# A reload that counted as a reader, the place of the second mixing, and one filter block evacuated by VectorE

## Chip, cores and metric

The kernel runs on one core of a Trainium2 chip. The metric is the device time of one execution in microseconds (us); a version is judged by the runs in the fast state only (here: within 1.5% of that kernel's fastest run), and all runs quoted here are of that state. A profile is one execution taken by the hardware profiler. Its span (about 2 us shorter than the time) is what the timelines count from.

## The reference, cut to what matters

```python
x = A_q                                             # [1, 2048, 640] bf16
g = sigmoid((x * gate_w).sum(-1, keepdims=True))
a = A(x, k, v, shift_k, ssm_k, ssm_D)               # 4-tap shift of k, times v, then a causal convolution
                                                    # of length 2048 over the sequence (FFT of length 4096), times q
b = B(x, w1, b1, w2, b2)                            # the MLP: layernorm, two matmuls over the sequence with a GELU between
return g * a + (1 - g) * b
```

The kernel does the FFT as matmuls with sine tables (TensorE) and butterflies ("mixing", VectorE). The sequence is in two halves, so almost everything in A exists twice.

Of the kernel before, what the change touches and what calls it, by code (L numbers as in the profile page):

```python
# [13 lines left out]
ALU = mybir.AluOpType  # L14
# [4 lines left out]
class _Tracker:  # L19
# [231 lines left out]
        self.dma_cnt[name] = 0  # L251

    def dma(self, stream, out_ap, in_ap, semname, transpose=False, noncontig=False, accum=False, wait=()):
        reads = [in_ap] + ([out_ap] if accum else []) + list(wait)
        writes = [out_ap]
        acc = self.pre(stream, reads, writes)
        engobj = self.eng[stream]
        sem = self.dma_sems[semname]
        if transpose:
            ins = engobj.dma_start_transpose(out_ap, in_ap)  # L260
        elif accum:
            ins = engobj.dma_start(out_ap, in_ap, accum_op=ALU.add, max_dma_last_dim=2560)  # L262
        elif noncontig:
            with self.nc.allow_non_contiguous_dma(reason="tiny"):
                ins = engobj.dma_start(out_ap, in_ap)
        else:
            ins = engobj.dma_start(out_ap, in_ap)
        ins.then_inc(sem, 16)
        self.dma_cnt[semname] += 16
        v = self.dma_cnt[semname]  # L270
        self.dma_hist[(semname, v)] = dict(self.known[stream])
        src = ("dma", semname, v)
        for reg, mode in acc:
            self.add_record(reg, mode, src)
        return v
# [234 lines left out]
def _build(nc, A_q, A_k, A_v, A_shift_k, A_ssm_k, A_ssm_D, B_x, B_w1, B_b1, B_w2, B_b2, gate_w, out):  # L510
    Bsz, S, D = A_q.shape
# [9 lines left out]
    with ExitStack() as es:  # L521
# [129 lines left out]
        def act(o, i, func, bias=None, scale=None, acc=None, vt=None, prio=None, name="act"):  # L651
            kw = {}
            rr = []
            nap = 0
            for k_, v_ in (("bias", bias), ("scale", scale)):
                if v_ is not None:
                    kw[k_] = v_
                    if isinstance(v_, bass.AP):
                        rr.append(v_)
                        nap += 1  # L660
            ww = [o]
            if acc is not None:
                kw["accum_out"] = acc
                ww.append(acc)

            def emit(s):
                src = i(s) if vt is not None else i
                return T.op("ACT", lambda e: e.activation(o, src, func, **kw), rr + [src], ww)  # L668
            return SC.add("ACT", act_dur(n_of(o), nap), emit, rr if vt is not None else rr + [i], ww, prio=prio, vt=vt, name=name)
# [31 lines left out]
        def dma(o, i, nbytes, stream="SP", prio=None, sem=None, rate=365.0, chain=False, **kw):  # L701
            if sem is None:
                sem = f"d{ndma[0]}"
                ndma[0] += 1
            if sem not in T.dma_sems:
                T.add_dma_sem(sem, es.enter_context(nc.semaphore(f"s_{sem}")))
            rd = [i] + ([o] if kw.get("accum") else []) + list(kw.get("wait", ()))
            o_ = SC.add(stream, nbytes / rate / 1000.0, lambda s: T.dma({"QA": "ACT"}.get(stream, stream), o, i, sem, **kw), rd, [o], prio=prio, lat=-1.0, name="dma")
            if chain:
                if last[0] is not None:  # L710
                    o_.after.add(last[0])
                last[0] = o_
            return o_
# [125 lines left out]
        def transp(h, db):  # L839
            vt = _VT("cv")  # L840
            items = []
            for kt in range(2):
                for p in range(4):
                    o = (lambda s, j=4 * kt + p: s[:, 128 * j:128 * j + 128])
                    dfold = h == 0 and kt == 0 and p == 0
                    if dfold:
                        items.append((o, ident[0:1, :], Drow[0:1, 128 * db:128 * db + 128], True, False))
                    items.append((o, V(ssm, db * S + 1024 * h + 4 * kt + p, [[8, 128]]), ident[:, :], not dfold, True))
            m_ = mms(vt, (spin(SPIN[db]) if h == 0 else []) + items, name="wtr")
            m_.dur = 0.5  # L850
            o_ = act(V(wT, 2 * h * SL + 128 * db, [[SL, 2], [D, 4], [1, 128]]), (lambda s: s[:, :].rearrange("q (a b c) -> q a b c", a=2, b=4)), ACT.Copy, vt=vt, name="wT")
            if h == 0:
                o_.after.add(sins[0 if db == 0 else 2])
# [85 lines left out]
        MIXP = 330  # L939
        LNA = 8  # L940
        lnlast = []
        kfirst = []
        KFP = (0, 5, 10, 15)
        srcW = lambda h: (lambda kt, p, ci: wT[:, 2 * h + kt, p, 320 * ci:320 * ci + 320])
        for h in range(2):
            for db in range(ND):
                transp(h, db)
            if h == 0:
                consts()
            if h in (1,):  # L950
                fwd_even(srcW(h), h, C[h], 1.0 / 1024.0, h == 1, "W")
            for p in (PORD if h not in (1,) else PORD[2:]):
                if h == 0 and p in (1, 3):
                    sins[p].prio = SC.ops[-1].idx - (16.5 if p == 1 else 8.5)
                fwd(srcW(h), h, p, C[h], p, 1.0 / 1024.0, "W", (lambda c, k2: False) if h == 0 else (lambda c, k2: c == 1))
            if h == 0:
                for t in range(8):
                    ln_tile(t // 4, t % 4)
                for t in range(8, 12):
                    ln_tile(t // 4, t % 4)  # L960
                lnlast.append(SC.ops[-1])
                ln_scale(0, LNA)
                ln_apply(0, LNA)
                lnlast.append(SC.ops[-1])
                for t in range(12, 16):
                    for o_ in ln_tile(t // 4, t % 4):
                        o_.after.update(lnlast[-1:])
                ln_scale(LNA, 16)
                ln_apply(LNA, 16)
                lnlast.append(SC.ops[-1])  # L970
                for g0 in KFP:
                    tt("POOL", KF[:, g0:g0 + 20 // len(KFP), :, :], V(cw, 7 * g0, [[7, 20 // len(KFP)], [1, 7], [0, 32]]), V(m32, 0, [[0, 20 // len(KFP)], [0, 7], [1, 32]]), ALU.mult, xr=[pv3] if g0 == 0 else []).after.update(kfirst[:1])
                    kfirst.append(SC.ops[-1])
                for hk in range(2):
                    k_turn(hk)
                mixing(C[0], SS, 0, fine=True, prio=MIXP)
            else:
                mixing(C[1], C[0], 0, conj=True, prio=MIXP)
# [152 lines left out]
        def H(hs, c):  # L1131
            h, s = hs
            return V(h, s * SL + 1280 * c, [[SL, 2], [1, 1280]])
# [54 lines left out]
                dma(comp(V1[g], i, 0), tmp, 128 * 5120, stream="POOL", prio=0, accum=True)  # L1188


        def invmix(Ya, Yb, sc, z0, z2):
            def sl(h, s):
                return V(h, s * SL, [[1, SL]])

            def pr(h, s, rev=False):
                return V(h, s * SL + (1280 if rev else 0), [[-1280 if rev else 1280, 2], [1, 1280]])
            (ha, sa), (hb, sb), (hs, ss) = Ya, Yb, sc
            tt("DVE", sl(hs, ss), sl(ha, sa), sl(ha, sa + 1), ALU.add)
            tt("DVE", sl(ha, sa), sl(ha, sa), sl(ha, sa + 1), ALU.subtract)
            tt("DVE", sl(hs, ss + 1), sl(hb, sb), sl(hb, sb + 1), ALU.add)  # L1200
            tt("DVE", sl(hb, sb), sl(hb, sb), sl(hb, sb + 1), ALU.subtract)
            tt("DVE", sl(ha, sa + 1), sl(hs, ss), sl(hs, ss + 1), ALU.add)
            tt("DVE", sl(hb, sb + 1), sl(hs, ss), sl(hs, ss + 1), ALU.subtract)
            oA = V(hs, ss * SL, [[SL + 1280, 2], [1, 1280]])
            oB = V(hs, (ss + 1) * SL, [[-1280, 2], [1, 1280]])
            tt("DVE", oA, pr(ha, sa), pr(hb, sb, True), ALU.add)
            tt("DVE", oB, pr(ha, sa), pr(hb, sb, True), ALU.subtract)
            return {0: (ha, sa + 1), 2: (hb, sb + 1), 1: (hs, ss), 3: (hs, ss + 1)}

        def inverse(h, Z):  # L1210
# [51 lines left out]
        acc_dma(A1[1], V1[1])  # L1262
        acc_dma(A1[0], V1[0])
        chained(product, A0[1], A0[1], V0[1], H(V0[1], 0))
        for kt in range(2):
            dma(q_hi[:, kt, :, :], dr(A_q, 512 * kt * D, [[4 * D, 128], [1, 4 * D]]), 128 * 5120, wait=[H(A0[1], 1)])
        chained(product, A0[0], A0[0], V0[0])
        for kt in range(2):
            dma(q_lo[:, kt, :, :], dr(A_q, (1024 + 512 * kt) * D, [[4 * D, 128], [1, 4 * D]]), 128 * 5120).after.add(w2last)
        Z0 = invmix(A0[0], A0[1], C3a, None, None)  # L1270
        inverse(0, Z0)
        Z1 = invmix(A1[0], A1[1], (SS, 0), None, None)
        inverse(1, Z1)

        SC.run()
# [35 lines left out]
```

## The kernel before: what the change touches

The kernel records every operation first. A list scheduler, working with modelled durations, then fixes the order on each engine; a tracker adds the semaphore waits from what each operation reads and writes. So a declared read acts twice: in the order and in the waits.

```python
# tracker: what a DMA is recorded to read
def dma(self, stream, out_ap, in_ap, semname, transpose=False, noncontig=False, accum=False, wait=()):
    reads = [in_ap] + ([out_ap] if accum else []) + list(wait)
    writes = [out_ap]
    acc = self.pre(stream, reads, writes)            # waits on the issuing stream
    # ... start the DMA
    for reg, mode in acc:
        self.add_record(reg, mode, src)              # later writers of these regions wait for this DMA
```

```python
# scheduler: the same regions once more
rd = [i] + ([o] if kw.get("accum") else []) + list(kw.get("wait", ()))
o_ = SC.add(stream, nbytes / rate / 1000.0, lambda s: T.dma(..., **kw), rd, [o], prio=prio, lat=-1.0, name="dma")
```

```python
def transp(h, db):                                   # half h, block db of 5: 8 transposes on TensorE
    # ...
    o_ = act(V(wT, ...), (lambda s: ...), ACT.Copy, vt=vt, name="wT")      # ScalarE evacuates 128x1024 fp32

def invmix(Ya, Yb, sc, z0, z2):                      # eight instructions of 128x2560
    (ha, sa), (hb, sb), (hs, ss) = Ya, Yb, sc
    tt("DVE", sl(hs, ss), sl(ha, sa), sl(ha, sa + 1), ALU.add)             # 1
    tt("DVE", sl(ha, sa), sl(ha, sa), sl(ha, sa + 1), ALU.subtract)        # 2
    tt("DVE", sl(hs, ss + 1), sl(hb, sb), sl(hb, sb + 1), ALU.add)         # 3
    tt("DVE", sl(hb, sb), sl(hb, sb), sl(hb, sb + 1), ALU.subtract)        # 4  overwrites A0's second half
    tt("DVE", sl(ha, sa + 1), sl(hs, ss), sl(hs, ss + 1), ALU.add)         # 5  -> first inverse block
    tt("DVE", sl(hb, sb + 1), sl(hs, ss), sl(hs, ss + 1), ALU.subtract)    # 6  -> second inverse block
    tt("DVE", oA, pr(ha, sa), pr(hb, sb, True), ALU.add)                   # 7  -> third
    tt("DVE", oB, pr(ha, sa), pr(hb, sb, True), ALU.subtract)              # 8  -> fourth

chained(product, A0[1], A0[1], V0[1], H(V0[1], 0))   # ends in an accumulating DMA into H(A0[1], 1)
for kt in range(2):                                  # reload q into q_hi; "wait" holds it behind that DMA
    dma(q_hi[:, kt, :, :], dr(A_q, ...), 128 * 5120, wait=[H(A0[1], 1)])
# ...
Z0 = invmix(A0[0], A0[1], C3a, None, None)
inverse(0, Z0)                                       # uses q_hi
Z1 = invmix(A1[0], A1[1], (SS, 0), None, None)
inverse(1, Z1)                                       # uses q_lo
```

## Time and profile before

| | before |
|---|---|
| time, median of six runs (lowest to highest) | 183.76 us (183.45 to 185.66) |
| span of the profile | 181.9 us |
| TensorE busy, VectorE busy | 173.2 us, 171.3 us |
| Z0's first instruction starts | 143.64 |
| Z0's sixth instruction ends, second inverse block starts | 158.11, 158.25 |
| TensorE idle just before that | 1.74 us |
| last VectorE instruction ends | 179.65 |

The first three runs, with a median of 184.76 us, were the ones known when the prediction was made. The lines themselves, and how to read them, are in the prediction.

### The profile page before, as it was taken

What the parts mean: (1) busy time and instruction counts of PE and PEld (TensorE: products, weight loads), DVE (VectorE), ACT (ScalarE), POOL (GpSimd) and SP (SyncE); (2) the same over time, 40 slices, a digit from 0 to 9 for tenths busy, and PEclk for the clock granted to TensorE, in tenths of its full rate; (3) what the DMA queues carried; (4) which work ended last, traced back from release to release, by engine and by line L of the source; (5) the groups of instructions that cost most, each with busy time, mean ns of one, the idle gap of its engine ahead of it and who ended that gap; (6) DMA issues with size and microseconds to landing.
All of it is one profiled execution on the core that took longest, in us unless ns stands there. A gap on an engine that the chain in (4) does not pass through costs nothing.

```text
span 181.9 us, 3336 instructions
## 1 busy us (share of the span) xinstructions
PE 173.2 (95%) x1380; PEld 129.3 (71%) x1381; DVE 171.3 (94%) x203; ACT 116.9 (64%) x176; POOL 45.3 (25%) x42
## 2 busy tenths in 40 slices
PE   7969998899999999999999999999999999699993
PEld 2636785586778677776777778888888887477772
DVE  7999895999999999999999899999999996999974
ACT  5798998899898999428999911322313225156760
POOL 4089404580000055000241101205252000041300
PEclk9999999999999999999999999999999999999999
DMA  5999999999999999998499799797999999146787
GB/s 159 376 410 370 389 269 200 266 397 300 213 262 269 176 279 234 230 229 220 110 269 260 147 180 349 143 216 236 189 194 227 204 241 416 66 76 144 123 258 271
DMA packets 38542, 43.51 MB, mean 239 GB/s; under 512 B 15867, under 2 KB 31360, under 8 KB 38528
## 3 DMA queue, kind: packets, MB, share of 16 engines
q1 hardware_dynamic: 33296, 32.16, 58.0%
q0 software_dynamic: 5200, 11.14, 35.2%
q8 instruction: 11, 0.18, 0.4%
q14 instruction: 3, 0.02, 0.0%
q10 hardware_dynamic: 32, 0.01, 0.0%
HBM read 25.87 MB, written 2.62 MB: 157 GB/s over the span
## 4 chain that ended last, share of the span: by engine, by line
PE 47%; ACT 19%; DVE 18%; DMA 11%; issue 3%; SPq 0%; DVEq 0%
PE pp L293 47%; DVE C L624 10%; DMA C<-SS 5%; DMA q_hi<-in_A_q_dram 5%; ACT C L668 5%; ACT gq L668 5%; DVE tm L624 4%; ACT FTB L668 3%; ACT wT L668 3%; DVE q_hi L624 2%; ACT ksh L668 2%; ACT GT L668 2%; DVE SS L624 1%; ACT L668 1%; DVE O L680 0%
## 5 line engine op out<-in xcount | busy, mean ns | idle before, releaser
L293 PE MATMUL pp<-X,ring 128*128 128x320 bf16 x384 | 55.4, 299 | 0.0
L624 DVE TENSOR_TENSOR C<-C 128x2560 bf16<-128x2560 bf16 (+2 forms) x37 | 54.5, 1521 | 0.3 <-DMA q_hi<-in_A_q_dram 0.3
L293 PE MATMUL pp<-GT,W 128*128 128x320 bf16 x384 | 52.8, 299 | 0.0
L293 PEld LDWEIGHTS pp<-GT,W 128*128 128x128 bf16 x384 | 43.5, 113 | 8.7
L293 PEld LDWEIGHTS pp<-X,ring 128*128 128x128 bf16 x384 | 37.4, 98 | 14.4
L668 ACT ACTIVATE C<-pp 128x640 bf16<-128x640 f32 x64 | 40.4, 724 | 4.7 <-PE pp L293 4.7
L668 ACT ACTIVATE O<-pp,c,omg 128x640 bf16<-128x640 f32 x15 | 13.2, 883 | 33.8 <-PE pp L293 33.8
L262 POOL DMA_DIRECT2D C<-C x8 | 10.9, 1610 | 41.9 <-DVE C L624 38.4
L293 PE MATMUL pp<-wT,FTB 128*128 128x320 bf16 x112 | 17.2, 299 | 2.6 <-ACT wT L668 1.5
L668 ACT ACTIVATE cgb<-pp,gg 128x640 bf16<-128x640 f32 x16 | 12.7, 793 | 8.5 <-PE pp L293 8.5
L293 PEld LDWEIGHTS pp<-wT,FTB 128*128 128x128 bf16 x112 | 10.5, 98 | 7.9 <-ACT wT L668 2.0
L668 ACT ACTIVATE GT<-pp,cc 128x640 bf16<-128x640 f32 x12 | 9.5, 795 | 9.0 <-PE pp L293 9.0
L293 PE MATMUL pp<-C,FTB 128*128 128x320 bf16 x96 | 13.5, 299 | 1.7 <-DVE C L624 1.7
L624 DVE TENSOR_TENSOR tm<-C,C 128x2560 bf16<-128x2560 bf16 (+1 forms) x7 | 14.3, 2057 | 0.0
L920 DVE BATCH_NORM_STATS2 stats<-X 128x6 f32<-128x320 bf16 x32 | 13.5, 462 | 0.0
L293 PEld LDWEIGHTS pp<-C,FTB 128*128 128x128 bf16 x96 | 9.3, 98 | 5.6 <-issue 2.0
L624 DVE TENSOR_TENSOR SS<-C 128x2560 bf16<-128x2560 bf16 x8 | 11.8, 1486 | 1.3 <-DMA C<-C 1.3
L262 POOL DMA_DIRECT2D C<-q_hi x6 | 5.9, 977 | 27.7 <-DVE C L624 13.2
L262 POOL DMA_DIRECT2D O<-q_hi x4 | 4.8, 1200 | 28.5 <-DVE q_hi L624 28.5
L668 ACT ACTIVATE gq<-gq 128x640 bf16<-128x640 bf16 x16 | 11.8, 739 | 0.0
L624 DVE TENSOR_TENSOR C<-tm 128x2560 bf16<-128x2560 bf16 (+1 forms) x9 | 10.6, 1191 | 0.1
L668 ACT ACTIVATE wT<-pp 128x1024 bf16<-128x1024 f32 x10 | 9.7, 1043 | 1.0 <-PE pp L293 1.0
(73 smaller groups left out, 200.4 us busy)
## 6 DMA issues: line engine op xcount, KB each, us to landing
ring<-in_B_w_dram SPq DMA_DIRECT2D x12, 512.0 KB, 9.9
W<-in_B_w_dram SPq DMA_DIRECT2D x12, 512.0 KB, 6.3
C<-C POOLq DMA_DIRECT2D x8, 640.0 KB, 10.5
X<-in_A_q_dram SPq DMA_DIRECT2D x4, 640.0 KB, 8.4
kn<-in_A_k_dram SPq DMA_DIRECT2D x4, 640.0 KB, 9.1
out_dram<-O SPq DMA_DIRECT2D x7, 320.0 KB, 3.0
C<-SS POOLq DMA_DIRECT2D x3, 640.0 KB, 11.5
ssm<-in_A_ssm_k_dram SPq DMA_DIRECT2D x3, 512.0 KB, 6.8
```

Of the source, the lines that this page charges most:

```text
L262: ins = engobj.dma_start(out_ap, in_ap, accum_op=ALU.add, max_dma_last_dim=2560)
L293: ins = self.nc.tensor.matmul(ps_ap, lhsT=lhsT, rhs=rhs, start=start, stop=stop, skip_group_check=True)
L624: o_ = SC.add(eng, d, lambda s: T.op(eng, lambda e: e.tensor_tensor(o, a, b, op), rd, [o]), rd, [o], prio=prio, name="tt")
L668: return T.op("ACT", lambda e: e.activation(o, src, func, **kw), rr + [src], ww)
L920: ops.append(SC.add("DVE", 0.38, (lambda o, i: lambda s: T.op("DVE", lambda e: e.bn_stats(o, i), [i], [o]))(o, i), [i], [o]))
```

## The change

The intent: hold the reload of q_hi back as before, but only on the stream that issues it; keep the second mixing (Z1) behind the first (Z0); and give VectorE the last filter block while GpSimd computes the second half of the layernorm's reciprocal square roots ("the roots", rstd in the lines).

```diff
     def dma(self, stream, out_ap, in_ap, semname, ..., wait=()):
-        reads = [in_ap] + ([out_ap] if accum else []) + list(wait)
+        reads = [in_ap] + ([out_ap] if accum else [])
         writes = [out_ap]
+        if wait:
+            self.pre(stream, list(wait), [])         # waits on the issuing stream, nothing recorded
         acc = self.pre(stream, reads, writes)
...
-            rd = [i] + ([o] if kw.get("accum") else []) + list(kw.get("wait", ()))
+            rd = [i] + ([o] if kw.get("accum") else [])
...
+            if h == 1 and db in [4]:
+                ow = V(wT, 2 * h * SL + 128 * db, [[SL, 2], [D, 4], [1, 128]])
+                def emit(s):
+                    src = s[:, :].rearrange("q (a b c) -> q a b c", a=2, b=4)
+                    return T.op("DVE", lambda e: e.tensor_copy(ow, src), [src], [ow])
+                SC.add("DVE", dve_dur(1024, 1), emit, [], [ow], prio=2, vt=vt, name="wTd").after.add(stlast[-1])
+                return
...
-        def invmix(Ya, Yb, sc, z0, z2):
+        def invmix(Ya, Yb, sc, bfirst=False, behind=None):
+            n0 = len(SC.ops)
...
+            for (hy, sy), k in (((hb, sb), 1), ((ha, sa), 0)) if bfirst else (((ha, sa), 0), ((hb, sb), 1)):
+                tt("DVE", sl(hs, ss + k), sl(hy, sy), sl(hy, sy + 1), ALU.add)
+                tt("DVE", sl(hy, sy), sl(hy, sy), sl(hy, sy + 1), ALU.subtract)
...
+            for o_ in SC.ops[n0:]:
+                o_.after.update(behind or ())
...
+        lastacc = SC.ops[-1]
-            dma(q_hi[:, kt, :, :], ..., wait=[H(A0[1], 1)])
+            dma(q_hi[:, kt, :, :], ..., wait=[H(A0[1], 1)]).deps.add(lastacc)
...
+        Z0 = invmix(A0[0], A0[1], C3a)
+        z0last = SC.ops[-1]
         inverse(0, Z0)
+        Z1 = invmix(A1[0], A1[1], (SS, 0), False, [z0last])
```

The flag bfirst is false in both calls, so of the mixing only the rule "behind" is new.

More of the change, by code (lines that the diff above doesn't have):

```diff
@@ L941, in _build @@
         lnlast = []
+        stlast = []
         kfirst = []
@@ L967, in _build @@
                         o_.after.update(lnlast[-1:])
+                stlast.append(SC.ops[-1])
                 ln_scale(LNA, 16)
@@ L1197, in invmix @@
             (ha, sa), (hb, sb), (hs, ss) = Ya, Yb, sc
-            tt("DVE", sl(hs, ss), sl(ha, sa), sl(ha, sa + 1), ALU.add)
-            tt("DVE", sl(ha, sa), sl(ha, sa), sl(ha, sa + 1), ALU.subtract)
-            tt("DVE", sl(hs, ss + 1), sl(hb, sb), sl(hb, sb + 1), ALU.add)
-            tt("DVE", sl(hb, sb), sl(hb, sb), sl(hb, sb + 1), ALU.subtract)
+            for (hy, sy), k in (((hb, sb), 1), ((ha, sa), 0)) if bfirst else (((ha, sa), 0), ((hb, sb), 1)):
+                tt("DVE", sl(hs, ss + k), sl(hy, sy), sl(hy, sy + 1), ALU.add)
+                tt("DVE", sl(hy, sy), sl(hy, sy), sl(hy, sy + 1), ALU.subtract)
             tt("DVE", sl(ha, sa + 1), sl(hs, ss), sl(hs, ss + 1), ALU.add)
@@ L1264, in _build @@
         chained(product, A0[1], A0[1], V0[1], H(V0[1], 0))
+        lastacc = SC.ops[-1]
+        assert lastacc.eng == "POOL"
         for kt in range(2):
-            dma(q_hi[:, kt, :, :], dr(A_q, 512 * kt * D, [[4 * D, 128], [1, 4 * D]]), 128 * 5120, wait=[H(A0[1], 1)])
+            dma(q_hi[:, kt, :, :], dr(A_q, 512 * kt * D, [[4 * D, 128], [1, 4 * D]]), 128 * 5120, wait=[H(A0[1], 1)]).deps.add(lastacc)
         chained(product, A0[0], A0[0], V0[0])
@@ L1269, in _build @@
             dma(q_lo[:, kt, :, :], dr(A_q, (1024 + 512 * kt) * D, [[4 * D, 128], [1, 4 * D]]), 128 * 5120).after.add(w2last)
-        Z0 = invmix(A0[0], A0[1], C3a, None, None)
+        Z0 = invmix(A0[0], A0[1], C3a)
+        z0last = SC.ops[-1]
         inverse(0, Z0)
-        Z1 = invmix(A1[0], A1[1], (SS, 0), None, None)
+        Z1 = invmix(A1[0], A1[1], (SS, 0), False, [z0last])
         inverse(1, Z1)
```

## The prediction

> **What bounds the kernel now.** I read the page first, for who is busy, and then only the two places that the change touches. Part 1 of the page of the kernel before:
>
> ```profile
> PE 173.2 (95%) x1380; PEld 129.3 (71%) x1381; DVE 171.3 (94%) x203; ACT 116.9 (64%) x176; POOL 45.3 (25%) x42
> ```
>
> TensorE and VectorE are both nearly full in a span of 181.9 us, so nothing can be gained but the gaps of these two, and closing a gap of one helps only while the other does not stand in the way. Next, therefore, the list of waits, for TensorE and then VectorE:
>
> ```profile
> PE pp L293 <- DVE C L624: 1.7, 1, 1.7
> PE pp L293 <- ACT wT L668: 1.5, 1, 1.5
> DVE X L639 <- POOL rstd L624: 2.7, 2, 2.1
> DVE SS L624 <- DMA C<-C: 1.3, 1, 1.3
> DVE C L624 <- DMA q_hi<-in_A_q_dram: 0.3, 1, 0.3
> ```
>
> TensorE's largest gap is 1.74 us, one wait for VectorE; its second, 1.55 us for wT, ends at 13.6 us in the trace, in the first half of the filter, which the change does not touch. The chain that ended last, from 133 us on in the order of time, tells why TensorE waited there:
>
> ```profile
> 133.98 9.76 DMA C<-SS
> ...
> 144.19 9.53 DMA q_hi<-in_A_q_dram
> ...
> 153.81 4.31 DVE C L624 x3
> 158.12 0.14 issue
> 158.25 20.82 PE pp L293 x152
> ```
>
> The reload of q_hi lands at 153.72; only then VectorE runs three instructions, and after the third TensorE starts and never stops again until 0.55 us of VectorE end the work. The last timeline is that of VectorE from 143 us on (start, length, what, idle time before):
>
> ```profile
> 143.64 4.30 DVE L624 TENSOR_TENSOR C<-C 128x2560 bf16<-128x2560 bf16 x3
> 147.85 1.49 DVE L624 TENSOR_TENSOR SS<-C 128x2560 bf16<-128x2560 bf16 x1
> 149.25 1.48 DVE L624 TENSOR_TENSOR C<-C 128x2560 bf16<-128x2560 bf16 x1
> 152.01 1.49 DVE L624 TENSOR_TENSOR SS<-C 128x2560 bf16<-128x2560 bf16 x1 [1.28 <-DMA C<-C]
> 153.81 4.30 DVE L624 TENSOR_TENSOR C<-C 128x2560 bf16<-128x2560 bf16 x3 [0.30 <-DMA q_hi<-in_A_q_dram]
> ```
>
> I read this against the code of invmix, which has eight instructions of this size for each half. The outputs to SS are the first and third of the second half (Z1); those to C are the first half (Z0) and Z1's second. The order is Z0's 1, 3 and 2; Z1's first; Z0's fifth (TensorE's inverse starts at 150.92 on it); Z1's third; Z0's fourth; Z1's second; Z0's sixth, for which TensorE waits. So the sixth of Z0 comes ninth. It was pushed back because the program counts the reload of q_hi as a reader of A0's second half, which Z0's fourth overwrites: a wait that no data need, since the reload reads the input in HBM.
>
> **What the Trainium skill says.** (1) "DMA: Bandwidth & Descriptors", Anatomy of one DMA: DMA engines do not wait on semaphores; the issuing sequencer does, before dispatch. So the wait that delays the reload can be put on the issuing stream alone. The trace agrees: the SP queue shows 11.8 us waiting on C<-SS, and the reload is issued at 143.80, right after C<-SS lands at 143.74. (2) "VectorE: DVE Perf Modes", The TRN2 errata: a PSUM to SBUF instruction costs 120 cycles plus its elements at 0.96 GHz on VectorE, 172 plus its elements at 1.2 GHz on ScalarE. For 1024 fp32 columns that is an estimate of 1.19 us and 1.00 us. The trace has ScalarE's at 1.04 us (4.70 us for five in a row, 0.94 each); it has no such VectorE copy, only 320-column PSUM instructions with a second operand at 552 ns, where the formula gives 458. I take 1.2 to 1.3 us. (3) "GPSIMD Engine Reference", Specifications: VectorE and GpSimd contend when VectorE runs a two-port mode or has two SBUF inputs. A copy from PSUM is neither, so the roots should keep their 1.66 us; no row of this trace shows such a pair. (4) "TensorE: Matmul & The Clock Gate", Part 1: back-to-back warm matmuls take N / 2.4 GHz plus 2.5 ns, 136 ns for 320 columns. The trace agrees: 16 of them from 150.92 to 153.10 are 136 ns each.
>
> **The change, part by part.**
>
> *Reload wait.* The wait stays on the issuing stream (same gate, same 143.8) but the reload no longer counts as a reader. Z0's fourth no longer waits. Removed: the 0.30 us wait and, more, the detour by which Z1's instructions stood before it.
>
> *Mixing order.* The flag bfirst is false in both calls, so the pairs stay in the old order. What is new is that all of Z1 must be placed after the start of Z0's eighth. Z0 then runs straight through. Instructions of 128x2560 follow one another at 1.43 us (4.30 for three). From 143.64: the fifth still ends near 150.7, the sixth at 143.64 + 6 x 1.42 = 152.2 instead of 158.1, the seventh 153.6, the eighth 155.0. Nothing is added: it is the same 16 instructions. Z1's third moves from 152 to after 156, so its 1.28 us wait for C<-C, which landed at 152, is gone too.
>
> TensorE after that: from 150.92 to its last matmul it has 152 + 24 + 16 = 192 left, of which 64 are MLP matmuls that can go anywhere, 192 x 0.136 = 26.1 us, so 177.0 at the best against 179.08 now. That includes the 1.74 us gap and small ones.
> VectorE after that: from 143.64 to 179.65 it has 33.1 us of busy time in 36.0, so about 176.8 at the best. It has to make Z0, four products with q_hi (0.75 each) and five of Z1 before TensorE's second inverse: 155.0 + 3.0 + 7.1 = 165.1. TensorE can fill until 150.92 + 64 x 0.136 (first inverse) + 40 x 0.136 (MLP but for the last tile) = 165.1. The two meet at the same time: no slack. So I take the gap of 1.74 us as won, less some tenths for this meeting: **about -1.5 us**.
>
> *The last filter block on VectorE.* In this window ScalarE evacuates five blocks while VectorE waits for the roots:
>
> ```profile
> 24.47 4.70 ACT L668 ACTIVATE wT<-pp 128x1024 bf16<-128x1024 f32 x5
> 27.86 0.21 DVE L924 BATCH_NORM_AGGREGATE mv<-stats 128x2 f32<-128x12 f32 x1
> 28.48 1.66 POOL L624 TENSOR_TENSOR rstd<-sd,cst 128x8 f32<-128x8 f32 x1
> 30.17 2.94 DVE L639 TENSOR_SCALAR X<-X,mv,rstd 128x640 bf16<-128x640 bf16 x8 [2.11 <-POOL rstd L624]
> ```
>
> ScalarE's fifth ends at 29.17. VectorE is free at 28.07, its copy would end at 28.07 + 1.2 = 29.3, before the roots at 30.14. So the block is ready no sooner, it is free on VectorE, and ScalarE has 0.94 us less to do in a place where it then sits idle for 0.88 us. TensorE fills the time with MLP matmuls (27.39 to 29.74) and shows no gap at its next filter matmul. After 30.17 VectorE is busy without a pause of note up to 143, and that start is set by the roots. I give this part **0, within 0.3 us**.
>
> Sum: -1.5 us of 184.76, so 183.2 us.
>
> **Rivals.** *TensorE runs out of filler.* If Z1's fifth is later than 165.1, the order made ahead of time puts the last MLP tile there, and the last inverse block then ends the work with its own tail: ScalarE 0.79, then VectorE 0.82, 0.49, 0.38 and twice 0.55, about 3.4 us after TensorE's inverse. For it: VectorE's best end (176.8) is as late as TensorE's. Against it: the last tile is last in priority. It would leave some 0.5 us of gain: 184.2. *The reload becomes the wait.* q_hi lands at 153.72 and its first product comes at about 155; if the reload were 2 us later it would stop VectorE. Against: its gate is unchanged; 1.3 us of margin. It would cost up to 1 us: 184. *Part three is worth more*: the program is put in order by a model of durations, and a changed step early can reorder all that follows. The small TensorE gaps from 30 to 37 us (0.52, 0.51, 0.24) could go, giving 182; or reordering could cost as much.
>
> **Range and chances.** The three runs before spread over 2.2 us, so the median alone moves by nearly a microsecond. With 0 to 2.5 us gain at the extremes I set 181.5 to 184.7. Faster by over 2% needs 3.7 us, more than all TensorE gaps that the change can reach (1.74 + 1.3): 0.05. Slower by over 2% needs a bad reordering: 0.03. Within 2%: 0.92.
>
> **What would show it.** Right: in the profile after, the wait of VectorE on q_hi and on C<-C is gone; eight instructions of Z0 stand together from about 144 to 155; TensorE's 1.74 us gap is gone; the reload is still issued right after C<-SS lands; one VectorE copy wT<-pp of 1.2 to 1.3 us stands in the gap at 28, with the 2.1 us wait shortened by it and the roots still at 1.66. Wrong: a new TensorE gap near 165, Z0 beginning later than 143.6, the copy pushing the normalization past 30.2, or TensorE's order before 140 changed so that gaps move elsewhere.

## The result

| | before | after |
|---|---|---|
| time, median of six runs | 183.76 us | 181.87 us (181.73 to 182.95) |
| ratio, 95% interval | 1 | 0.9883 (0.9836 to 0.9931) |
| span of the profile | 181.9 us | 180.9 us |
| Z0's first instruction to the last VectorE instruction | 143.64 to 179.65 = 36.01 us | 144.59 to 178.82 = 34.23 us |

A ratio here is the mean time of one kernel's runs over the mean of the other's in the same rounds, so not quite the ratio of the medians. The result is an improvement of 1.2%, within 2% of before. The profiled execution of the changed kernel was the slowest of its six. Two early loads landed late in it: the first filter load at 7.39 us, for which TensorE waited 1.19 us, and a load of X, for which VectorE waited 1.09 us until 9.00. VectorE's later work is about 1 us late (0.95 us at Z0's start). So I compare lengths, not times from the start.

Part 1 of the page of the changed kernel, and the end of its chain of work that ended last (start, length, what):

```profile
PE 173.7 (96%) x1381; PEld 128.7 (71%) x1381; DVE 172.4 (95%) x204; ACT 116.1 (64%) x175; POOL 44.2 (24%) x42
```

```profile
42.12 136.13 PE pp L295 x1048
178.25 0.03 issue
178.27 0.55 DVE O L682
```

The busy times have hardly moved; the idle ones have. Before, the last part of the chain passed through two DMAs (C<-SS, then the reload of q_hi) and VectorE to TensorE; now it is one run of TensorE from 42 us to the end, without a pause. VectorE's timeline at the place of the old wait:

```profile
144.59 8.50 DVE L626 TENSOR_TENSOR C<-C 128x2560 bf16<-128x2560 bf16 x6
...
153.13 2.90 DVE L626 TENSOR_TENSOR C<-C,C 128x2560 bf16<-128x2560 bf16 x2
...
155.94 0.82 DVE L626 TENSOR_TENSOR q_hi<-cgb,q_hi 128x1280 bf16<-128x1280 bf16 x1
...
156.67 1.49 DVE L626 TENSOR_TENSOR SS<-C 128x2560 bf16<-128x2560 bf16 x1
```

Six and two instructions of Z0 stand together with no wait; then the first product with q_hi, also without a wait; only then the first of Z1. Of the list of waits, the first and the last were there before (2.7 and 0.9 us); the two between are new, the late loads of this execution:

```profile
DVE X L641 <- POOL rstd L626: 1.6, 2, 1.0
...
PE pp L295 <- DMA ssm<-in_A_ssm_k_dram: 1.2, 1, 1.2
...
DVE stats L929 <- DMA X<-in_A_q_dram: 1.1, 1, 1.1
...
DVE cgb L626 <- ACT cgb L670: 0.7, 2, 0.5
```

VectorE's waits for C<-C and for q_hi are gone, and so is TensorE's 1.7 us for VectorE. Last, the timeline at the copy:

```profile
29.07 1.17 DVE L857 CAST wT<-pp 128x1024 bf16<-128x1024 f32 x1
...
29.56 1.66 POOL L626 TENSOR_TENSOR rstd<-sd,cst 128x8 f32<-128x8 f32 x1
...
30.30 0.25 PEld L295 LDWEIGHTS pp<-wT,FTB 128*128 128x128 bf16 x3 [0.32 <-DVE wT L857]
...
31.26 2.94 DVE L641 TENSOR_SCALAR X<-X,mv,rstd 128x640 bf16<-128x640 bf16 x8 [1.02 <-POOL rstd L626]
```

The copy fits into VectorE's wait for the roots (2.11 us before, 1.02 us now). The roots beside it take their 1.66 us. Weight loads even waited 0.32 us for it, so the block was ready no sooner than by ScalarE.

### The profile page after: what moved, and what is told of

It is laid out like the page before. It is cut to its first block, busy times and chain, and to the rows that moved or that the text cites. A ratio compares the mean times of both kernels' runs of the same rounds, so it can differ in the third digit from the quotient of the medians.

```text
span 180.9 us, 3335 instructions
## 1 busy us (share of the span) xinstructions
PE 173.7 (96%) x1381; PEld 128.7 (71%) x1381; DVE 172.4 (95%) x204; ACT 116.1 (64%) x175; POOL 44.2 (24%) x42
## 4 chain that ended last, share of the span: by engine, by line
PE 87%; ACT 7%; DMA 3%; DVE 0%; issue 0%; SPq 0%
PE pp L295 87%; DMA ssm<-in_A_ssm_k_dram 3%; ACT C L670 2%; ACT ksh L670 2%; ACT wT L670 2%; ACT L670 1%; ACT FTB L670 1%; ACT GT L670 0%; DVE O L682 0%; SPq L269 0%; ACT cw L670 0%
## 5 line engine op out<-in xcount | busy, mean ns | idle before, releaser
L670 ACT ACTIVATE ksh<-pp 128x1024 bf16<-128x1024 f32 (+1 forms) x12 | 9.8, 894 | 0.6 <-PE pp L295 0.6
L626 POOL TENSOR_TENSOR KF<-cw,m 128x1120 bf16<-128x1120 bf16 x4 | 8.1, 2064 | 8.2 <-DVE pint L640 8.2
```

Of the source, the lines that this page charges most:

```text
L626: o_ = SC.add(eng, d, lambda s: T.op(eng, lambda e: e.tensor_tensor(o, a, b, op), rd, [o]), rd, [o], prio=prio, name="tt")
L670: return T.op("ACT", lambda e: e.activation(o, src, func, **kw), rr + [src], ww)
```

## The experiments

Nine kernels were run with five rounds each, every one with results equal to the reference within its tolerance. Comparing the programs instruction by instruction made sure of what each edit changes in the order; the traces agree, by operation and tile, wherever an order is called the same below. The theory: the false reader cost the time, through the order that it forced more than through the wait. Rivals: the wait itself, the mixing rule, or the copy is what gains.

| kernel | median us | ratio to before (95%) |
|---|---|---|
| e_tail: no copy | 181.86 | 0.9887 (0.9849 to 0.9925) |
| e_wtd: the copy alone | 183.94 | 1.0005 (0.9973 to 1.0037) |
| e_reload: the reload wait alone | 182.10 | 0.9898 (0.9863 to 0.9932) |
| e_behind: the mixing rule alone | 186.39 | 1.0140 (1.0096 to 1.0183) |
| e_oldplace_nowait: old order, wait gone | 183.61 | 1.0001 (0.9981 to 1.0020) |
| e_newplace_oldwait: new order, wait back | 189.71 | 1.0329 (1.0300 to 1.0359) |
| e_nobehind: changed, no mixing rule | 181.87 | 0.9895 (0.9879 to 0.9912) |
| e_nogate: changed, reload not held back | 183.40 | 0.9976 (0.9961 to 0.9992) |
| e_wtd_both: changed, one more block on VectorE | 183.89 | 1.0005 (0.9991 to 1.0019) |

**e_tail: the change without the copy.**

```diff
-            if h == 1 and db in [4]:
+            if h == 1 and db in []:
```

> The change without its copy on VectorE: new reload wait and new mixing order, all five filter blocks on ScalarE. TensorE's order is the same as in the changed kernel; the only difference is the one copy. Theory (the gain is in the tail): ratio to the kernel before 0.986 to 0.991, the same as the whole change within 0.3 us; in the profile TensorE's 1.74 us gap before the second inverse block is gone. Rival (the copy early on carries a good part of it): a ratio of 0.994 or more.

TensorE's timeline around the first inverse blocks of this kernel:

```profile
150.70 8.86 PE L295 MATMUL pp<-C,FTB 128*128 128x320 bf16 x64
159.40 5.60 PE L295 MATMUL pp<-GT,W 128*128 128x320 bf16 x40
```

Four inverse blocks run together without a gap. The ratio is that of the whole change, so the copy is not what gains; and by the traces TensorE and VectorE run the same sequence as before up to 147 us, so the gain is in the tail.

**e_wtd: the copy alone.** The reload wait and the mixing are as before:

```diff
-        reads = [in_ap] + ([out_ap] if accum else [])
+        reads = [in_ap] + ([out_ap] if accum else []) + list(wait)
...
-            rd = [i] + ([o] if kw.get("accum") else [])
+            rd = [i] + ([o] if kw.get("accum") else []) + list(kw.get("wait", ()))
...
-        Z1 = invmix(A1[0], A1[1], (SS, 0), False, [z0last])
+        Z1 = invmix(A1[0], A1[1], (SS, 0), False, None)
```

> The copy on VectorE alone; reload wait and mixing order as before. Theory: within 0.3 us of the kernel before (ratio 0.998 to 1.002), TensorE's 1.74 us gap stays, VectorE's wait for the roots shrinks from 2.1 to 1.0 us. Rival (the freed 0.94 us of ScalarE counts): faster by 0.5 to 1 us, ratio 0.995 or less.

```profile
158.15 2.33 PE L295 MATMUL pp<-C,FTB 128*128 128x320 bf16 x16 [1.89 <-DVE C L626]
```

The gap in TensorE's timeline stays (1.89 us here) and the time is that of before. The copy is worth nothing that these runs resolve (their interval is 0.3% to either side, about 0.6 us).

**e_reload: the reload wait alone.** No copy (as in e_tail) and no mixing rule:

```diff
-        Z1 = invmix(A1[0], A1[1], (SS, 0), False, [z0last])
+        Z1 = invmix(A1[0], A1[1], (SS, 0), False, None)
```

> The new reload wait alone; no rule that holds the second mixing behind the first, all filter blocks on ScalarE. In this order one instruction of the second mixing stands between the sixth and the seventh of the first, so the seventh comes 1.4 us later, and TensorE has 8 MLP matmuls in between. Theory (it is the false reader that cost the time): ratio 0.986 to 0.992, no TensorE gap over 0.3 us after 140 us. Rival (the mixing rule is needed as well): a gap of 1 us or more stays, ratio 0.995 or more.

```profile
151.23 4.51 PE L295 MATMUL pp<-C,FTB 128*128 128x320 bf16 x32
155.58 1.25 PE L295 MATMUL pp<-GT,W 128*128 128x320 bf16 x8
```

The seventh of Z0 is later by one instruction, and TensorE fills the time with eight MLP matmuls, without a gap. Its ratio is 0.9898 against 0.9887 of e_tail, which has the rule as well; the intervals overlap almost wholly.

**e_behind: the mixing rule alone.** The first two hunks of e_wtd, and no copy.

> The mixing rule alone: the second mixing behind the first, but the reload of q_hi still counts as a reader. Now nothing of the second mixing may fill the time until q_hi has landed (about 153.7). Theory: VectorE stands still for some 4 us before the fourth instruction of the first mixing, and the kernel is slower than before by 1.5 to 4 us, ratio 1.008 to 1.022. Rival (the mixing order is what gains): faster, ratio below 0.995.

VectorE's timeline, then TensorE's, of this kernel:

```profile
154.67 3.02 DVE L626 TENSOR_TENSOR C<-C 128x2560 bf16<-128x2560 bf16 x2 [4.25 <-DMA q_hi<-in_A_q_dram]
```

```profile
157.84 2.33 PE L295 MATMUL pp<-C,FTB 128*128 128x320 bf16 x16 [2.53 <-DVE C L626]
...
165.44 5.05 PE L295 MATMUL pp<-GT,W 128*128 128x320 bf16 x36
...
179.28 1.79 PE L295 MATMUL pp<-GT,W 128*128 128x320 bf16 x12
```

Without Z1's instructions to fill the wait, VectorE stands still for 4.25 us. The kernel is 1.4% slower: the detour in the old order was the scheduler's remedy for the false wait, and without the remedy the false wait costs more. The scheduler also put twelve of the last MLP tile's 24 matmuls before the second inverse (in the stretch of 36), which leaves only twelve behind the last inverse block. How the loss divides between the wait and this order was not tested.

**e_oldplace_nowait: the old order, the wait gone.** Every instruction of every engine is in the place it has in the kernel before; only the wait on the chip is gone. No copy and no rule, and in the scheduler:

```diff
-            rd = [i] + ([o] if kw.get("accum") else [])
+            rd = [i] + ([o] if kw.get("accum") else []) + list(kw.get("wait", ()))
```

> The kernel before with every instruction in its old place on every engine; only the semaphore wait of VectorE for the reload of q_hi is gone on the chip. Theory (the order cost more than the wait itself): a gain of 0.3 us or less, ratio 0.998 to 1.000, and TensorE's gap before the second inverse block stays at 1.4 to 1.7 us. Rival (the wait itself was the cost): the gap falls below 0.5 us, ratio 0.993 or less.

```profile
158.10 2.33 PE L295 MATMUL pp<-C,FTB 128*128 128x320 bf16 x16 [1.39 <-DVE C L626]
```

TensorE's gap shrinks by 0.35 us and the ratio is 1.0001, with an interval of 0.2% to either side (0.37 us). The wait itself was worth at most about that. This and e_reload carry the theory: the same false reader, removed from the order too, gives the whole gain.

**e_newplace_oldwait: the new order, the wait back.** The changed kernel in every place, but the tracker records the read again:

```diff
-        reads = [in_ap] + ([out_ap] if accum else [])
+        reads = [in_ap] + ([out_ap] if accum else []) + list(wait)
```

> The changed kernel with every instruction in its new place, but on the chip VectorE waits for the reload of q_hi again before the first write to A0's second half. Theory: VectorE stands still from about 149 to 154.5, about 4 to 5 us; slower than the changed kernel by 2.5 to 4.5 us, ratio to the kernel before 1.002 to 1.013. Rival (VectorE catches up, the wait is hidden): within 0.5 us of the changed kernel.

VectorE's timeline; then TensorE's; then the table of stretches (start:end, length, busy us and count of TensorE, weight loads, VectorE, ScalarE and GpSimd, granted TensorE clock, DMA share, GB/s):

```profile
154.35 4.30 DVE L626 TENSOR_TENSOR C<-C 128x2560 bf16<-128x2560 bf16 x3 [5.50 <-DMA q_hi<-in_A_q_dram]
```

```profile
157.39 11.35 PE L295 MATMUL pp<-C,FTB 128*128 128x320 bf16 x64 [5.39 <-DVE C L626]
```

```profile
156.00:157.00 1.00, 0.00 (x0) 0.00 (x0) 1.00 (x1) 0.00 (x0) 0.00 (x0) 0.50 0.42 172
...
161.00:162.00 1.00, 1.00 (x6) 0.56 (x4) 0.57 (x1) 0.15 (x1) 0.00 (x0) 0.50 0.00 0
...
163.00:164.00 1.00, 1.00 (x10) 0.73 (x8) 1.00 (x2) 0.66 (x1) 0.20 (x1) 1.00 0.00 0
```

My direction was right and my size was a miss: I had expected 2.5 to 4.5 us more than the changed kernel, and it is 7.8 us. The gap of TensorE is 5.39 us, the size of VectorE's wait, since in this order the fifth of Z0, which the first inverse block needs, also stands behind the fourth. The rest is a second effect: the clock granted to TensorE fell to 0.50 during the gap and stayed there until about 162.5 us. The 64 matmuls took 11.35 us instead of 8.86 us, 2.5 us more. The two together are 7.9 us. The Trainium skill, "TensorE: Matmul & The Clock Gate", Part 1, says this: after one idle window of about 3.4 us the clock goes to half rate, and sustained work of such a window brings it back; the window is free-running. The case agrees: the gaps of 1.74 us (before) and 2.53 us (e_behind) kept the clock at 1.00 through the gap and the matmuls after it, the gap of 5.39 us halved it. The trace has the clock at 0.50 from 155.68 to 162.50 us: 6.83 us, the length of two such windows. The matmuls, which began at 157.39 us, fell into the middle of the first, so only the second was busy from end to end.

**e_nobehind: the changed kernel without the mixing rule** (the edit of e_reload, with the copy kept).

> The changed kernel without the mixing rule (reload wait and VectorE copy stay). Theory: the rule is worth nothing beside the new wait, so the time is that of the changed kernel within 0.3 us, ratio 0.986 to 0.991. Rival: the seventh instruction of the first mixing comes too late and costs 0.5 us or more.

The median is 181.87 us, the same as the changed kernel. Beside the new reload wait the rule does nothing that can be measured.

**e_nogate: the reload not held back at all.** The order of TensorE, VectorE, ScalarE and GpSimd is that of the changed kernel; the reload goes out at 121.2 and 132.5 us instead of near 144.

```diff
-            dma(q_hi[:, kt, :, :], ..., wait=[H(A0[1], 1)]).deps.add(lastacc)
+            dma(q_hi[:, kt, :, :], ...)
```

> The changed kernel with no gate on the reload of q_hi at all: it goes out as soon as the buffer is free (after the accumulating transfers that read it, near 130 us) and stands before the last W2 load on the queue. Everything else is in the same place. Theory: with the false reader gone the gate is only there for order, and the time is that of the changed kernel within 0.5 us. Rival (the gate keeps the reload from slowing the accumulating transfers that VectorE needs next): those land later, VectorE or TensorE waits 1 us or more, slower by 0.5 to 2 us.

The chain, then VectorE's and TensorE's timelines of this kernel:

```profile
133.98 12.55 DMA C<-SS
```

```profile
146.55 7.10 DVE L626 TENSOR_TENSOR C<-C 128x2560 bf16<-128x2560 bf16 x5 [1.42 <-DMA C<-SS]
```

```profile
152.40 8.85 PE L295 MATMUL pp<-C,FTB 128*128 128x320 bf16 x64 [1.31 <-DVE C L626]
```

The rival is right and my theory was not. The accumulating transfer C<-SS, issued at the same 133.98 us as before, takes 12.55 us instead of 9.76, because it shares the DMA engines with an early reload: while it was under way, the queue that carries SyncE's loads moved 1.18 MB, against 0.52 MB before, and the 0.66 MB between them are one reload of 640 KB. VectorE needs it for Z0's third instruction and waits 1.42 us, TensorE 1.31 us. The time is 1.5 us above the changed kernel's. So the gate is of use on the issuing stream, and only there.

**e_wtd_both: a copy where VectorE has no gap.** The last block of the first half goes to VectorE as well:

```diff
-            if h == 1 and db in [4]:
+            if db in [4]:
...
-                SC.add("DVE", ..., name="wTd").after.add(stlast[-1])
+                SC.add("DVE", ..., name="wTd").after.update(stlast[-1:] if h == 1 else [])
```

> The changed kernel, and the last block of the first half of the filter goes to VectorE too, near 12 us, where VectorE has no gap. TensorE's wait for wT at 13 us (0.8 to 1.5 us) should shrink to 0.5 us or less. Theory (VectorE and TensorE meet with no slack at the first inverse block, so VectorE's time outside its gap costs in full): VectorE is about 1.1 us later at that place, TensorE gets a gap of 1 us or more there, and the kernel is slower than the changed one by 0.4 to 1.5 us, ratio to the kernel before 0.991 to 0.998. Rival (TensorE alone is the bound): faster than the changed kernel by 0.4 to 1 us, ratio 0.986 or less.

```profile
160.29 7.23 PE L295 MATMUL pp<-GT,W 128*128 128x320 bf16 x52
167.35 4.51 PE L295 MATMUL pp<-C,FTB 128*128 128x320 bf16 x32
...
176.05 1.79 PE L295 MATMUL pp<-GT,W 128*128 128x320 bf16 x12
```

It is slower than the changed kernel by 2.0 us, somewhat more than I expected, and in another way. Z0 starts at 144.35 us, against 143.42 in e_tail, whose start was not late either: 0.9 us later. TensorE's wait at 13 us did shrink, from 1.40 us (e_tail) to 0.62, not quite the 0.5 expected. I had expected a gap of TensorE at the first inverse block; there is none. Instead the order changed, and not only there: TensorE's order differs from the changed kernel's in many places from about 12 us on. So this run shows that the version is slower, not what the copy alone costs. In the tail the scheduler spent 52 MLP matmuls (40 in the changed kernel) before the second inverse, twelve of them from the last tile, so the last inverse block ends the work with its own tail. The chain of this kernel shows the tail (start, length, what):

```profile
176.25 0.80 ACT cgb L670
177.07 0.84 DVE cgb L626
177.94 0.49 DVE O L626
178.43 0.31 DVE cgb L640
178.76 0.55 DVE O L682
```

No version that beats the changed kernel came out of these runs; e_tail and e_nobehind equal it with less code.

## Why the prediction held, and where it was off

- **What held TensorE up: right.** The trace gives the sum: the sixth of Z0 ended at 158.11; take away three instructions of Z1 (3 x 1.42), the 1.28 and the 0.30 us of waits, and it is 152.27. In the changed kernel it ended at 153.09, less the late start of 0.95: 152.14. TensorE had hidden all but 1.74 us of these 5.9 us behind MLP matmuls and the first inverse block.
- **The wait against the detour: right.** "Removed: the 0.30 us wait and, more, the detour": e_oldplace_nowait (nothing) and e_reload (all of it) show it.
- **The mixing rule: overrated in the text.** I wrote Z0's straight run to its account, "Z0 then runs straight through". e_reload and e_nobehind show that the reload wait alone gives it but for one instruction, which TensorE fills.
- **The size: a little low.** I expected -1.5 us, the 1.74 us "less some tenths for this meeting". From Z0 to the end the traces differ by 1.78 us, the medians by 1.9 us. The meeting near 165 us did come: Z1's fifth ended at 166.0 us and TensorE started on it at 166.12, but without a gap in the matmuls, with only 0.26 us at the weight loads. The deduction was the mis-sized term. The forecast time, 183.2 us, is 1.3 us above the measured 181.87; 1.0 us of that is the base, since the three runs known then had a median of 184.76 us and all six have 183.76.
- **The copy: right, at zero.** It took 1.17 us (I took 1.2 to 1.3; the formula cited in the prediction gives an estimate of 1.19), inside the wait for the roots, and the roots kept their 1.66 us beside it, as the prediction took from the Trainium skill, "GPSIMD Engine Reference", Specifications. e_wtd and e_tail bound it from both sides.
- **The rivals.** The filler did not run out in the changed kernel, but it did in e_behind and e_wtd_both, in the way described; the tail that the prediction puts at "about 3.4 us" is 3.58 us by its own terms, and 3.56 us in e_wtd_both (176.21 to 179.77). The reload did not become the wait: its first product came without one. The early order did not change; e_tail has the very order of the changed kernel on TensorE.
- **Signs of being wrong that did appear.** In the profiled execution Z0 begins at 144.59, later than 143.6, and the normalization at 31.26, later than 30.2. Both go with its late loads and not with the copy: e_wtd, with the same copy and no late load, has 143.37 and 30.06.

## What to carry to other kernels

When a dependency is declared only to hold a transfer back, put it on the stream that issues the transfer; declared as a read it also delays whoever writes that region next, and a scheduler that plans around it can cost more than the wait on the chip. Removing a wait in a fixed order may gain nothing (e_oldplace_nowait) and forcing an order without removing the wait may lose (e_behind): change both together, and test them apart. With two engines near 95% busy, look for a gap in the trace before moving work to one of them: inside VectorE's gap the copy cost nothing here; a second one outside it, with the new order that the scheduler made of it, lost 2 us (e_wtd_both).

## What the Trainium skill lacked or had wrong

- "VectorE: DVE Perf Modes", The TRN2 errata: its formula for fp32 from PSUM (120 cycles plus elements, an estimate of 1.19 us for 1024) agrees with the copy's 1.17 us. It has no row for an instruction with a second operand from SBUF: for the 128x320 one the same formula would give an estimate of 0.46 us, and the trace has 0.55.
- "DMA: Bandwidth & Descriptors" has no duration for an accumulating transfer from SBUF to SBUF. Its fit for transfers issued by GpSimd (2.0 us plus bytes at 436 GB/s; an estimate of 3.5 us for 640 KB) has no term for other transfers under way and cannot stand in for C<-SS here: 9.76 us with the DMA engines fully busy with this and other transfers, 12.55 us with an early reload among them.
